# Linear attention with a gated convolution on one core: batch 0's softmax of q by additions in SBUF, batch 1's attention in float32, and a new order of all steps

## The chip, the core and the metric

The kernel runs on one core of one Trainium2 chip. The core has five engines that run side by side, each working through its own instructions strictly in the order in which they were issued: TensorE (PE, matrix products; its weight loads are shown apart as PEld), VectorE (DVE), ScalarE (ACT), GpSimd (POOL) and SyncE (SP), which here only issues DMA transfers. The metric is the device time of one execution in microseconds (us). Three runs of the kernel before gave a median of 322.0 us (321.49 to 322.12).

## What is computed

Eight batches, eight heads, 576 positions (`S`), 64 features per head (`D`), so 512 channels (`C`). All inputs and the output are float32.

```python
q_s = softmax(q, axis=-1)                 # over the 64 features of a head
k_s = softmax(k, axis=2)                  # over the 576 positions
kv  = einsum('bhsd,bhse->bhde', k_s, v)   # 64x64 per head
x   = einsum('bhsd,bhde->bhse', q_s, kv)  # -> (batch, 576, 512)
gate = sigmoid(causal_conv(x, conv_w))    # five taps per channel along the positions
out  = (gate * (x @ w_val)) @ w_out       # two 512x512 products
```

The softmaxes subtract the maximum first and divide by the sum plus 1e-9.

## The kernel before

The two large products are split into three passes each: both operands are cut into a high part (`fp32r`) and the rest, and low x high, high x high and high x low are added up in PSUM (`split_product`, L542). One step `value b m` or `project b m` makes one block of 128 channels of one batch with 24 such matmuls of 288 columns; a batch has four of each.

A batch goes through these stages. Loads of k, q and v. The softmax of k: for batches 0 and 1 from a copy that has channels on the partitions (`load_kc`, `k_top`, `k_raise`, `k_turn`), for the others by maxima of the channels (`load_km`, `k_peak`, L274) that go through memory and come back spread over the partitions (`k_row`, `k_spread`), a subtraction in five parts (`k_sub`, L289) and an exponential (`k_exp`). The softmax of q: maxima (`q_max`, L347), subtraction, exponential, sums (`q_sum`, L362), scaling in four or five parts (`q_mul`, L387 and L389). `kv` (L433) makes the 64x64 blocks, `kv_norm` scales them. `q_turn` transposes q on PE, `q_turned` copies the result to SBUF, and `attend b p` (L498, L499) makes x for 128 channels in PSUM. x is read from PSUM by `x_high` and `x_low` (the two parts for the product), by `first` (the last tap) and four `tap` steps (L524 on DVE; in the other form L527 on ACT and L528 on POOL). After that come `sigmoid`, `value`, `gated` (L563), `g_high` and `g_low` (L571), `project`, and `store`.

PSUM has two buffers of tag `x` and two of tag `mm`. `q_turn` and `attend` take turns in the first pair, so an `attend` can only begin when every reader of an earlier x in its buffer has ended.

The softmax of q in batch 0 is done on PE before the change. `q_peak` transposes the maxima, `q_top` copies them to SBUF, `q_lift` copies q into PSUM by a product with the identity, `q_minus` adds the negative maxima, and `q_raise` takes the exponential out of PSUM. Batch 1 uses `q_neg` and `q_exps` instead: a negated maximum, then either an addition on POOL and one exponential on ACT (letter p), or eight exponentials with a bias on ACT (letter a).

The weights come as pairs of 32-bit words and are put together on the way (`load_words`, `part`, `field`, `scaled`, `signed`, `joined`, then `w_high` and `w_low`): index 0 to 3 are blocks of `w_val`, 4 to 7 of `w_out`, 8 the taps.

In batches listed in `F32_BATCHES` the attention is one float32 product; in the others `kv_high`, `kv_low` and `q_low` cut the operands in two parts and `attend` makes three passes.

What sets the order is a list, `ORDER`, written out by hand: each entry is a step with its batch, its block and, where there is a choice, its engine (a ACT, v DVE, p POOL). The steps are issued in that order, so the place of an entry decides the place of its instructions on their engines, its DMAs in SP's queue among them. `warm n` takes a PSUM buffer and makes n transposes of the identity in it.

## Time and profile before

| what | value |
|---|---|
| median of three runs | 322.0 us |
| the profiled execution, its own time | 320.3 us |
| its span, first to last instruction | 318.5 us |
| mean granted TensorE clock | 0.995 |
| HBM read, written | 41.39 MB, 9.45 MB |
| instructions | 6426 |

The span is what all views of the trace are measured from. The 1.8 us between it and the execution's own time lie around it. A row of a view gives a line of the kernel, an engine, an operation, the tile written and the tiles read; x is a count, the first number the busy time in us, the second the mean in ns of one instruction. A value in square brackets is idle time of the engine ahead of the row with what ended it.

### The profile page before, as it was taken

To read this page: it belongs to the slowest core of one execution; us is meant where nothing else is said; L and a number is where in the kernel's file an instruction comes from. 1 tells how busy PE (TensorE), PEld (TensorE's weight loads), DVE (VectorE), ACT (ScalarE), POOL (GpSimd) and SP (SyncE) were. 2 spreads that over 40 slices of the span, in tenths; PEclk is the share of its full clock that TensorE was granted. 3 is DMA by queue.
4 is the path that set the end of the run, shared out by engine and by line. 5 is a ranking of instruction groups with operands and counts; after the bars stand their busy time and mean duration, and the time that the engine had idled before them with its cause. 6 is when DMAs were issued, how large, how long until landed. Compare 5 with 4: busy or idle time off the path is not lost.

```text
span 318.5 us, 6426 instructions
## 1 busy us (share of the span) xinstructions
PE 297.3 (93%) x2557; PEld 276.4 (87%) x2557; DVE 271.5 (85%) x374; ACT 204.6 (64%) x316; POOL 188.7 (59%) x157
## 2 busy tenths in 40 slices
...
GB/s 250 370 390 174 410 396 199 194 8 175 238 264 264 74 181 139 254 189 112 143 64 313 50 232 283 160 16 355 82 0 37 39 77 2 0 74 76 0 42 108
DMA packets 20525, 51.25 MB, mean 161 GB/s; under 512 B 2832, under 2 KB 7312, under 8 KB 17808
## 3 DMA queue, kind: packets, MB, share of 16 engines
...
q8 instruction: 20, 0.33, 0.4%
q14 instruction: 9, 0.07, 0.1%
HBM read 41.39 MB, written 9.45 MB: 160 GB/s over the span
## 4 chain that ended last, share of the span: by engine, by line
PE 55%; DVE 19%; DMA 16%; issue 4%; ACT 4%; SPq 1%; DVEq 0%; ACTq 0%
PE out L542 22%; PE val L542 20%; DVE gate L524 5%; DMA km<-in_k_strided 5%; PE x L498 4%; PE kv L433 4%; DMA words<-in_w_out 3%; DMA out<-o 2%; DMA q<-in_q 2%; DMA q<-in_q_tail 2%; PE qTps L465 2%; DVE qm L347 2%; DVE g L563 2%; DVE qs L362 2%; DVE kpk L274 2%
## 5 line engine op out<-in xcount | busy, mean ns | idle before, releaser
L524 DVE SCALAR_TENSOR_TENSOR gate<-x,cw,gate 128x575 f32<-128x575 f32 (+3 forms) x99 | 78.0, 807 | 3.3 <-POOL gate L528 1.5
L528 POOL TENSOR_TENSOR gate<-gate,far 128x572 f32<-128x572 f32 (+3 forms) x29 | 39.5, 1363 | 39.2 <-ACT far L527 38.9
L542 PE MATMUL out<-gh,w_out_lo 128*128 128x288 f32 x256 | 57.0, 301 | 0.7 <-ACT gh L160 0.7
L542 PE MATMUL val<-xh,w_val_lo 128*128 128x288 f32 x256 | 56.5, 302 | 0.8 <-DVE o L162 0.7
L542 PE MATMUL out<-gl,w_out_hi 128*128 128x288 f32 x256 | 55.6, 296 | 0.9 <-DVE gl L571 0.9
L542 PE MATMUL val<-xl,w_val_hi 128*128 128x288 f32 x256 | 55.0, 296 | 0.9 <-DVE xl L518 0.9
L542 PE MATMUL out<-gh,w_out_hi 128*128 128x288 f32 x256 | 55.4, 295 | 0.0
L542 PE MATMUL val<-xh,w_val_hi 128*128 128x288 f32 x256 | 54.8, 295 | 0.0
L571 POOL TENSOR_TENSOR gl<-g,gh 128x576 fp32r<-128x576 f32 x25 | 36.8, 1476 | 29.5 <-ACT gh L160 23.1
L542 PEld LDWEIGHTS out<-gl,w_out_hi 128*128 128x128 f32 x256 | 41.4, 188 | 1.4 <-DVE gl L571 1.4
L542 PEld LDWEIGHTS val<-xh,w_val_lo 128*128 128x128 f32 x256 | 40.9, 188 | 1.8 <-DVE o L162 0.9
L542 PEld LDWEIGHTS val<-xl,w_val_hi 128*128 128x128 f32 x256 | 41.2, 188 | 1.2 <-DVE xl L518 1.2
L542 PEld LDWEIGHTS out<-gh,w_out_lo 128*128 128x128 f32 x256 | 41.2, 189 | 1.0 <-ACT gh L160 1.0
L542 PEld LDWEIGHTS out<-gh,w_out_hi 128*128 128x128 f32 x256 | 41.5, 188 | 0.0
L542 PEld LDWEIGHTS val<-xh,w_val_hi 128*128 128x128 f32 x256 | 41.3, 188 | 0.0
L389 POOL TENSOR_TENSOR q<-q,qs 128x512 f32<-128x512 f32 x25 | 26.2, 1070 | 14.7 <-DVE qs L364 14.7
L563 DVE TENSOR_TENSOR g<-val,gate 128x576 f32<-128x576 f32 x32 | 23.9, 749 | 9.9 <-PE val L542 7.3
L527 ACT ACTIVATE far<-x,cw 128x572 f32<-128x572 f32 (+3 forms) x29 | 21.0, 737 | 14.2 <-DVE gate L524 9.3
L160 ACT CAST gh<-g 128x576 fp32r<-128x576 f32 x25 | 16.7, 672 | 17.5 <-DVE g L563 17.4
L160 ACT COPY o<-out 128x576 f32<-128x576 f32 (+1 forms) x22 | 13.5, 618 | 22.1 <-PE out L542 12.1
L531 ACT ACTIVATE gate<-gate 128x576 f32<-128x576 f32 x32 | 21.6, 685 | 6.1 <-DVE gate L524 3.5
L289 POOL TENSOR_TENSOR k<-k,kmax 128x512 f32<-128x512 f32 x18 | 24.9, 1397 | 0.9 <-DMA kmax<-krow 0.9
(103 smaller groups left out, 590.1 us busy)
## 6 DMA issues: line engine op xcount, KB each, us to landing
...
```

Of the source, the lines that this page charges most:

```text
L160: nc.scalar.copy(out=out, in_=in_)
L289: engine(e).tensor_sub(kk[r, cs], kk[r, cs], mx[r, cs])
L389: engine(e).tensor_mul(qq, qq, s.unsqueeze(2).broadcast_to([P, H, D]))
L433: nc.tensor.matmul(acc[h * D:(h + 1) * D, p, :], T["k", b][:, c, cs] if c < 4 else ktz[b % 2][:, cs], T["v", b][:, c, hd] if c < 4 else T[ ...
L498: nc.tensor.matmul(ps[:, :MAIN], a, z, start=(i == 0), stop=(i == len(parts) - 1))
L524: nc.vector.scalar_tensor_tensor(out=a, in0=x, scalar=w, in1=a, op0=ALU.mult, op1=ALU.add)
L527: nc.scalar.activation(part, x, AF.Copy, scale=w)
L528: nc.gpsimd.tensor_add(a, a, part)
L531: nc.scalar.activation(T["gate", b, p], T["gate", b, p], AF.Sigmoid)
L542: nc.tensor.matmul(ps[:, cs], a[:, kb, ms], z[kb][:, cs], start=(kb == 0 and i == 0), stop=(kb == NB - 1 and i == 2),)
L563: nc.vector.tensor_mul(T["g", b, m], T["val", b, m], T["gate", b, m])
L571: engine(e).tensor_sub(T["gl", b, m], T["g", b, m], T["gh", b, m].bitcast(F32))
```

## The change

Four things change. Batch 0's q goes the way that batch 1's goes: the five functions for PE and the tile `minus` are taken out, `q_neg` and `q_exps` are used for batch 0 too. `F32_BATCHES` becomes `(0, 1)`, so batch 1 has no `kv_high`, `kv_low` or `q_low`, and its four `attend` steps are one float32 pass. Steps with one input may name POOL as their engine: `part` 2, 4 and 6, `scaled` 2, `w_high` 0, 1 and 5, `kv_high` three times and `g_high` eleven times do. And `ORDER` is another list throughout: 40 `tap` steps in the ACT and POOL form where there were 29, ten `q_mul` on ACT where there were four, and every engine's instructions in another sequence.

```diff
-F32_BATCHES = (0,)
+F32_BATCHES = (0, 1)
 ORDER = [step.strip() for step in """
-    load_kc 0 1, load_q 0 0 2, load_words 8, k_top 0 1, load_ident, q_lift 0 0, q_max 0 0 2, q_peak 0 0 2,
...
+    load_kc 1 0, load_words 8, field 8, load_kc 0 2, k_top 0 2, scaled 8 a, k_raise 0 2, k_top 1 0, load_words 1,
...
     def load_ident():
         nc.sync.dma_start(out=ident, in_=ident_in)
-        nc.scalar.mul(minus, ident[:H, :H], -1.0)
...
-    def q_peak(b, c0=0, c1=5):
-        c1 = min(c1, q_parts(b))
-        ps = T["qpk", b, c0] = bank(f"qpk_{b}_{c0}", "x")
-        for c in range(c0, c1):
-            nc.tensor.transpose(ps[:H, (c - c0) * P:(c - c0 + 1) * P], T["qm", b][:, c * H:(c + 1) * H], ident)
-
-    def q_top(b, c0=0, c1=5, e="a"):
...
-    def q_lift(b, g):
-        ps = T["qlps", b, g] = bank(f"qlps_{b}_{g}", "x")
-        for i, c in enumerate(q_group(b, g)):
-            nc.tensor.matmul(ps[:, i * C:(i + 1) * C], ident, T["q", b][:, c], start=True, stop=False)
-
-    def q_minus(b, g):
...
-    def q_raise(b, g):
-        c = q_group(b, g)
-        nc.scalar.activation(T["q", b][:, c[0]:c[-1] + 1], T["qlps", b, g][:, :len(c) * C].rearrange("p (c n) -> p c n", n=C), AF.Exp)
...
-    minus = const.tile([H, H], F32, tag="minus", name="minus")
```

Three places of the new order follow, as it was and as it is. First SP's queue up to batch 0's v, the first that `kv 0` needs last. Names carry batch and block: `kc_0_3` is block 3 of batch 0, `words3` the third block of `w_val`, `vt0` the tail of v for batches 0 and 1. Before:

```order
L222 DMA words1_113<-in_w_val 128x4x256
L301 DMA kc_0_3_115<-in_k_channels 128x576
L196 DMA q0_92<-in_q 128x1024
L198 DMA q0_92<-in_q_tail 128x512
L222 DMA words3_125<-in_w_val 128x4x256
L301 DMA kc_0_2_138<-in_k_channels 128x576
L301 DMA kc_1_1_142<-in_k_channels 128x576
L196 DMA q1_147<-in_q 128x2048
L222 DMA words0_152<-in_w_val 128x4x256
L301 DMA kc_1_2_165<-in_k_channels 128x576
L202 DMA v0_170<-in_v 128x2080
L205 DMA vt0_172<-in_v_tail 128x520
```

After:

```order
L196 DMA q0_118<-in_q_tail 128x512
L194 DMA q0_118<-in_q 128x1024
L298 DMA kc_0_1_132<-in_k_channels 128x576
L194 DMA q1_138<-in_q 128x2048
L220 DMA words2_143<-in_w_val 128x4x256
L298 DMA kc_1_2_146<-in_k_channels 128x576
L223 DMA ident_72<-in_ident 128x128
L220 DMA words4_175<-in_w_out 128x4x256
L220 DMA words0_200<-in_w_val 128x4x256
L298 DMA kc_1_3_202<-in_k_channels 128x576
L200 DMA v0_229<-in_v 128x2080
L203 DMA vt0_231<-in_v_tail 128x520
```

Ahead of v0 there now stand two more blocks of weights (five in all with `words1` and `words3`, which come just above these rows) and one more `kc`; `ident` has moved from the fourth place of the queue to the fifteenth.

Second, VectorE from the first tap of batch 0 on (`gate_0_1` is block 1 of batch 0; the widths 575 to 572 tell the taps 3 to 0 apart). Before:

```order
L524 SCALAR_TENSOR_TENSOR gate_0_1_385<-x_0_1_381,cw_74,gate_0_1_385 128x575
L524 SCALAR_TENSOR_TENSOR gate_0_1_385<-x_0_1_381,cw_74,gate_0_1_385 128x574
L524 SCALAR_TENSOR_TENSOR gate_0_1_385<-x_0_1_381,cw_74,gate_0_1_385 128x573
L518 TENSOR_TENSOR xl_0_1_419<-x_0_1_381,xh_0_1_387 128x576
L524 SCALAR_TENSOR_TENSOR gate_0_1_385<-x_0_1_381,cw_74,gate_0_1_385 128x572
L524 SCALAR_TENSOR_TENSOR gate_0_0_417<-x_0_0_399,cw_74,gate_0_0_417 128x575
L518 TENSOR_TENSOR xl_0_0_437<-x_0_0_399,xh_0_0_421 128x576
L524 SCALAR_TENSOR_TENSOR gate_0_0_417<-x_0_0_399,cw_74,gate_0_0_417 128x574
L524 SCALAR_TENSOR_TENSOR gate_0_0_417<-x_0_0_399,cw_74,gate_0_0_417 128x573
L249 TENSOR_SCALAR e4_350<-e4_350 128x512
L250 SCALAR_TENSOR_TENSOR e4_350<-words4_348,e4_350 128x512
L524 SCALAR_TENSOR_TENSOR gate_0_0_417<-x_0_0_399,cw_74,gate_0_0_417 128x572
```

After:

```order
L490 SCALAR_TENSOR_TENSOR gate_0_1_386<-x_0_1_374,cw_73,gate_0_1_386 128x575
L490 SCALAR_TENSOR_TENSOR gate_0_1_386<-x_0_1_374,cw_73,gate_0_1_386 128x574
L484 TENSOR_TENSOR xl_0_1_417<-x_0_1_374,xh_0_1_388 128x576
L490 SCALAR_TENSOR_TENSOR gate_0_0_406<-x_0_0_394,cw_73,gate_0_0_406 128x575
L490 SCALAR_TENSOR_TENSOR gate_0_0_406<-x_0_0_394,cw_73,gate_0_0_406 128x574
L484 TENSOR_TENSOR xl_0_0_429<-x_0_0_394,xh_0_0_414 128x576
L490 SCALAR_TENSOR_TENSOR gate_0_0_406<-x_0_0_394,cw_73,gate_0_0_406 128x573
L271 TENSOR_REDUCE kpk_2_439<-km_2_2_408 128x1
L490 SCALAR_TENSOR_TENSOR gate_0_0_406<-x_0_0_394,cw_73,gate_0_0_406 128x572
L490 SCALAR_TENSOR_TENSOR gate_0_2_489<-x_0_2_484,cw_73,gate_0_2_489 128x575
```

Of block 1 two taps have left VectorE, and one of block 2 (its tap 2); the pair of `signed` that stood inside block 0's taps has moved behind them, and the first maximum of batch 2's k (`kpk_2`) stands there instead.

Third, GpSimd from the subtraction in batch 2's q (`q2`, `qm_2`) to that in batch 2's k (`k2`, `kmax_2`). Before:

```order
L351 TENSOR_TENSOR q2_372<-q2_372,qm_2_689 128x512
L262 TENSOR_TENSOR w_out_lo_78<-f5_518,w_out_hi_77 128x4x128
L571 TENSOR_TENSOR gl_0_1_769<-g_0_1_722,gh_0_1_739 128x576
L254 TENSOR_TENSOR f7_724<-e7_590,f7_724 128x512
L351 TENSOR_TENSOR q2_372<-q2_372,qm_2_689 128x512
L254 TENSOR_TENSOR f6_776<-e6_747,f6_776 128x512
L351 TENSOR_TENSOR q2_372<-q2_372,qm_2_689 128x512
L262 TENSOR_TENSOR w_out_lo_78<-f6_776,w_out_hi_77 128x4x128
L351 TENSOR_TENSOR q2_372<-q2_372,qm_2_689 128x512 x2
L528 TENSOR_TENSOR gate_1_1_773<-gate_1_1_773,far_1_1_0_854 128x572
L262 TENSOR_TENSOR w_out_lo_78<-f7_724,w_out_hi_77 128x4x128
L289 TENSOR_TENSOR k2_693<-k2_693,kmax_2_815 128x512 x2
```

After:

```order
L348 TENSOR_TENSOR q2_554<-q2_554,qm_2_682 128x512 x2
L537 TENSOR_TENSOR gl_0_1_735<-g_0_1_688,gh_0_1_711 128x576
L166 TENSOR_SCALAR f6_738<-words6_384 128x512
L251 TENSOR_TENSOR f6_738<-e6_639,f6_738 128x512
L494 TENSOR_TENSOR gate_1_1_725<-gate_1_1_725,far_1_1_3_769 128x575
L259 TENSOR_TENSOR w_out_lo_77<-f6_738,w_out_hi_76 128x4x128
L348 TENSOR_TENSOR q2_554<-q2_554,qm_2_682 128x512
L251 TENSOR_TENSOR f7_816<-e7_635,f7_816 128x512
L348 TENSOR_TENSOR q2_554<-q2_554,qm_2_682 128x512
L259 TENSOR_TENSOR w_out_lo_77<-f7_816,w_out_hi_76 128x4x128
L286 TENSOR_TENSOR k2_307<-k2_307,kmax_2_855 128x512 x4
L286 TENSOR_TENSOR kt2_372<-kt2_372,kmax_2_855 64x512
```

`TENSOR_SCALAR f6` is a step that ScalarE had. Batch 2's subtraction of q stands between the weights' last steps (`f6`, `f7`, `w_out_lo`) in both; the five instructions of `k_sub` now follow in one run.

More of the change, by code (lines that the diff above doesn't have):

```diff
@@ L68 @@
-    g_high 1 1 a, tap 1 3 0 v, g_low 1 1 v, sigmoid 1 2, value 1 2, gated 1 2, load_km 4 0, warm 0, tail_turn 2,
-    kv_high 2 a, q_turn 2 0, k_sub 3 0 v, k_peak 4 0, tail_turned 2 a, sigmoid 1 3, q_turn 2 1, load_v 3,
-    q_turned 2 0 a, g_low 1 0 p, g_high 1 2 a, q_turned 2 1 a, q_low 2 0, k_sub 3 4 p, load_q 3, kv_low 2 p,
-    g_low 1 2 p, value 1 3, attend 2 1, q_low 2 1, attend 2 0, x_high 2 1 a, gated 1 3, q_max 3, first 2 1 a,
-    g_high 1 3 a, first 2 0 a, k_sub 3 1 p, load_km 4 2, tap 2 0 3 v, x_low 2 1, tap 2 0 2 v, g_low 1 3 p,
@@ L93 @@
-    q_turn 4 0, k_sub 5 3 p, tap 3 3 0 v, q_sub 5 2 p, q_turn 4 1, kv_norm 4 v, kv_high 4 v, value 3 2,
-    q_turned 4 0 a, tail_turned 4 a, kv_low 4 p, value 3 3, q_sub 5 3 p, q_turned 4 1 a, g_low 3 0 p, k_peak 6 1,
-    sigmoid 3 3, q_low 4 0, gated 3 2, q_low 4 1, attend 4 0, gated 3 3, first 4 0 a, attend 4 1, load_km 7 3,
-    g_high 3 2 v, load_q 6, x_high 4 0 a, g_high 3 3 v, g_low 3 2 p, first 4 1 v, q_exp 5, load_k 6, g_low 3 3 p,
-    tap 4 1 3 a, tap 4 0 3 v, x_low 4 0, project 3 2, tap 4 1 2 a, tap 4 0 2 v, x_high 4 1 a, project 3 1,
@@ L133 @@
[L133 to L135 removed]
+    load_kc 1 0, load_words 8, field 8, load_kc 0 2, k_top 0 2, scaled 8 a, k_raise 0 2, k_top 1 0, load_words 1,
+    load_words 3, field 1, signed 8, scaled 1 a, load_kc 0 0, load_kc 0 3, load_q 0 2 5, field 3, part 1 a, signed 1,
```

202 lines of the change are left out of this document (99 added, 103 removed).

## The prediction

> **What bounds the kernel now.** I read the page's busy times first, then the busy time of three stretches.
>
> ```profile
> PE 297.3 (93%) x2557; PEld 276.4 (87%) x2557; DVE 271.5 (85%) x374; ACT 204.6 (64%) x316; POOL 188.7 (59%) x157
> 0.00:45.50 45.50, 33.54 (x277) 20.69 (x277) 37.97 (x66) 35.45 (x65) 22.25 (x26) 0.96 0.90 327
> 45.50:120.60 75.10, 70.22 (x624) 66.79 (x622) 69.06 (x90) 56.10 (x94) 57.70 (x47) 1.00 0.61 188
> 120.60:318.50 197.90, 193.50 (x1660) 188.88 (x1660) 164.50 (x220) 113.00 (x160) 108.72 (x85) 1.00 0.32 112
> ```
>
> The stretches give PE, PEld, DVE, ACT and POOL busy in turn, then clock, DMA share and GB/s. From 120.6 us on PE is busy 193.5 of 197.9 us: little but less matmul work could gain there. Up to 45.5 us DVE is the fullest compute engine (37.97 us), and the DMA engines are 90% busy. Between them PE is the bound, with holes. So the time is the arrival of the first `value`, plus PE's work, plus the holes. The PE timeline shows the arrival and the holes:
>
> ```profile
> 45.55 0.52 PE L542 MATMUL val<-xh,w_val_lo 128*128 128x288 f32 x2
> 65.59 0.53 PE L542 MATMUL out<-gh,w_out_lo 128*128 128x288 f32 x2 [0.65 <-ACT gh L160]
> 67.27 0.54 PE L542 MATMUL out<-gl,w_out_hi 128*128 128x288 f32 x2 [0.90 <-DVE gl L571]
> 82.31 0.54 PE L542 MATMUL val<-xl,w_val_hi 128*128 128x288 f32 x2 [0.93 <-DVE xl L518]
> 84.30 0.53 PE L542 MATMUL val<-xh,w_val_lo 128*128 128x288 f32 x2 [0.66 <-DVE o L162]
> 112.81 0.73 PE L498 MATMUL x<-qT,kvs 128*128 128x512 f32 x2 [1.14 <-ACT far L527]
> ```
>
> The chain that ended last, in order of time, gives what PE's work costs when nothing holds it: 48 matmuls 6.40 us (so a `value` or `project` 3.20), a `kv` 2.48, 16 transposes 1.75, an `attend` 0.70 + 0.17.
>
> ```profile
> 118.10 2.48 PE kv L433 x80
> 120.58 3.41 PE val L542 x24
> 153.50 6.40 PE val L542 x48
> 162.97 1.75 PE qTps L465 x16
> 171.12 0.70 PE x L498 x3
> 171.82 0.17 PE x L499 x2
> ```
>
> From the first `value` (45.55) to batch 2's first (120.58) lie 75.0 us. Both orders have the same steps in it: 16 `value` or `project` (51.2), two `kv` (5.0), four `q_turn` (3.5), a tail (0.4), eight `attend` (7.0), in sum 67.1. So **7.9 us are holes**. The five waits shown are 4.3 of them; the other 3.6 are small waits and restarts. 45.55 and 7.9 are what a new order can change.
>
> **Removed matmuls: 0.** The two large groups of batch 0's q matmuls kept PE busy 6.9 and 5.0 us:
>
> ```profile
> L411 PE MATMUL qlps<-q,ident 128*128 128x512 f32 x10 | 6.9, 825 | 5.7 <-DMA ident<-in_ident 5.7
> L416 PE MATMUL qlps<-minus,qtop 8*128 8x512 f32 x10 | 5.0, 616 | 0.6 <-DVE e L240 0.6
> ```
>
> They lie before 45.5 us, where PE idles 12 us; DVE's work and the loads hide them. Without that cover they would be worth some 12 us.
>
> **Arrival of the first value: -0.7 us.** `value 0 0` follows `attend 0 3`, which waits until block 0's last tap has left its PSUM buffer; so DVE's work up to that tap counts.
>
> ```profile
> 3.62 0.75 DVE L307 TENSOR_REDUCE ktop<-kc 128x1 f32<-128x576 f32 x1 [3.62 <-DMA kc<-in_k_channels]
> 43.59 1.53 DVE L524 SCALAR_TENSOR_TENSOR gate<-x,cw,gate 128x572 f32<-128x572 f32 x2
> 28.46 0.86 DVE L448 TENSOR_TENSOR kvd<-kv,ks 64x256 f32<-64x256 f32 x2
> L249 DVE TENSOR_SCALAR e<-e 128x512 int32<-128x512 int32 x8 | 3.3, 416 | 0.0
> L250 DVE SCALAR_TENSOR_TENSOR e<-words,e 128x512 int32<-128x512 int32 x8 | 5.5, 692 | 0.3
> L162 DVE COPY qtop<-qpk 8x256 f32<-8x256 f32 x1 | 0.4, 412 | 1.0 <-PE qpk L395 1.0
> L274 DVE TENSOR_REDUCE kpk<-km 128x1 f32<-128x576 f32 x24 | 17.7, 742 | 4.1 <-DMA km<-in_k_strided 4.1
> L389 DVE TENSOR_TENSOR q<-q,qs 128x512 f32<-128x512 f32 x7 | 4.8, 684 | 0.0
> L162 DVE CAST qT<-qTps 128x1024 fp32r<-128x1024 f32 x1 | 1.2, 1225 | 0.1
> taps<-in_conv_w SPq DMA_DIRECT2D x1, 20.0 KB, 3.8
> ```
>
> It loses two taps (a pair 1.53), one `signed` (0.42 + 0.69), the scalings of `kv_norm 0` (0.86) and `q_top` (0.41): 3.9. It gains a `k_peak` (0.74), `part` 3 and 8 (0.42 for the large one, by the one-input row of the same shape; the small one I put at 0.15), a `q_mul` (0.68) and a `q_turned` (1.23): 3.2. A small conversion that goes and two negations that come I set equal. Net -0.7. DVE now begins when the taps have landed, about 5.0 us (issued second, 3.8 to land), and not at 3.6; that costs 1.4. The 1.0 us wait for `qpk` goes, and I take 0.4 of the other early waits as swallowed too: together zero.
>
> The loads cost nothing as long as this cover holds:
>
> ```profile
> 12.00:16.00 4.00, 3.77 (x14) 2.48 (x14) 3.93 (x6) 3.42 (x5) 2.53 (x2) 0.57 1.04 419
> 11.84 1.79 PE L319 MATMUL kps<-ident,kc 128*128 128x128 f32 x8
> 21.26 1.04 PE L319 MATMUL kps<-ident,kc 128*128 128x128 f32 x8
> 30.00 1.13 PE L498 MATMUL x<-qT,kvd 128*128 128x512 f32 x2
> 35.75 2.51 DVE L524 SCALAR_TENSOR_TENSOR gate<-x,cw,gate 128x575 f32<-128x575 f32 x3
> 47.20 1.83 ACT L451 ACTIVATE kvd<-kv,ks 64x64 f32<-64x64 f32 x8
> ```
>
> Ahead of `vt0` stand 1312 KB more, at 419 GB/s 3.2 us. `kv 0` followed the transposes of 21.26, at 22.3, with v just landed; now it can begin at 25.5 to 26. With `kv` (2.48), `kv_norm` on ACT (1.83, as batch 1's) and the two ACT steps ahead of that, the first `attend` comes at about 31.9, not 30.0. But DVE reaches its first tap at 35.75 before, and by adding up its new list at 35.8 after. Nearly 6 us of cover shrink to 4, less the 2 or so that `first` and `x_high` need. If it goes, that tap is late next, and with it all of DVE.
>
> **Batch 1 in float32: +1.0 us.**
>
> ```profile
> 39.71 1.12 PE L498 MATMUL x<-qT,kvd 128*128 128x512 f32 x2 [0.70 <-DVE gate L524]
> 40.67 0.33 PE L499 MATMUL x<-qTt,kvd 128*128 128x64 f32 x2
> ```
>
> One float32 pass took 40.67 - 39.71 = 0.96 us on PE, three split passes 0.70. Four times 0.26 is 1.04, all on the bound. In return two `q_low` leave DVE and a `kv_low` leaves POOL; that goes into the holes.
>
> **Holes: 7.9 becomes 5.9, -2.0 us.** I went along PE's new order and asked at each step when its last input is there.
>
> ```profile
> L571 POOL TENSOR_TENSOR gl<-g,gh 128x576 fp32r<-128x576 f32 x25 | 36.8, 1476 | 29.5 <-ACT gh L160 23.1 <-DVE gh L162 6.4
> L389 POOL TENSOR_TENSOR q<-q,qs 128x512 f32<-128x512 f32 x25 | 26.2, 1070 | 14.7 <-DVE qs L364 14.7
> L289 POOL TENSOR_TENSOR k<-k,kmax 128x512 f32<-128x512 f32 x18 | 24.9, 1397 | 0.9 <-DMA kmax<-krow 0.9
> L605 POOL MEMSET kvd<- 128x512 f32 x2 | 1.0, 526 | 0.3 <-POOLq L645 0.3
> ```
>
> `project 0 0` still waits: batch 2's `q_max` stands on DVE ahead of `gated 0 1`, and POOL does two subtractions of q (1.07 each) before `g_low 0 1` (1.48). I make that 2.3 us, against 1.55 in the rows of 65.59 and 67.27. The waits at 82.31 and 84.30 go: the store that held a buffer is on ACT, and DVE has two `q_low` and two taps less. The one at 112.81 goes too: the ACT tap that frees the buffer now has a `project` between it and the `attend`. A new one stands at `kv 3`: from the first `value` to the last `k_sub 3` POOL has 55 us to do (15 sums or products of q 16, six `g_low` 9, ten `k_sub` 13, the weights 12, a tap, `kv_low` and two `g_high` 5), is 4 us behind at the start and waits 4 us for inputs that I can name; `kv 3` is then ready 1.5 us after PE gets there. So 2.3 + 1.5 + 0.2 of small ones, and about half of the unexplained 3.6: 5.9.
>
> One-input work on POOL is in no row. It lies between a fill (0.53) and a two-input pass (1.48), as far from the one as from the other, so I take 1.0. Four such steps on this path make the ends -1.9 and +1.9 us.
>
> [...]
>
> **After 120.6 us: 0.** The work is the same; 4.4 us of idle PE are there to lose or gain. DVE has fewer taps, POOL more in hand: no sign that I can defend.
>
> **Sum:** -0.7 + 1.04 - 2.0 = -1.7. The span of 318.5 becomes 316.8, the profiled execution's 320.3 becomes 318.6; the median of the runs shown is 322.0, so I predict **320.3**.
>
> **Rivals.** (1) *Slower: POOL becomes the bound.* It was busy 57.7 of 75.1 us, and my path leaves it 4 us of waiting. If one input costs 1.48 (+1.9) and it waits 4 more, `kv 3` comes 5.9 later, of which holes elsewhere on PE take up some 1.5: 324.7. Past 1.7 us of such delay the change is slower than before. For it: long waits such as `g_low`'s 29.5. Against: the old order left POOL time to wait; much of that was no need.
>
> (2) *PE's clock is low at the start.* The eight transposes took 1.79 us where the granted clock was 0.57, and 1.04 later. PE now begins with them at about 19 us. At that ratio `kv 0` and q's transposes take 3 us longer, of which 2 are covered, and what follows may lose another: +1 to +2, 321.3 to 322.3. Against: 12 us of idle PE before 45.5 left the clock at 0.96 on average.
>
> [...]
>
> (3) *The holes close*, down to the 2.0 unexplained: -3.9 more, 316.4. (4) *The change doesn't do at the start what it says*: the loads, not DVE, set the first `value`, and the taps that left DVE free nothing; v's 3.2 us less 2 of cover give +1.2 in place of -0.7: 322.2.
>
> **How the numbers follow.** Forecast 0.40, (1) 0.25, (2) 0.10, (3) 0.18, (4) 0.07. A measurement of this kernel tells 0.2%, 0.64 us, from no change. Faster beyond that: three quarters of the forecast, all of (3), some of (2): 0.52. Within: most of (2) and (4), a little of the forecast: 0.18. Slower: (1) and the rest, 0.30. The range leaves out a tenth at each end: 316.0 to 324.5.
>
> **What would show it.** First `value` at 44.9; `kv 0` at 25.5 to 26; batch 2's first `value` at 118.9; batch 1's `attend` at 0.96 + 0.17; no wait before batch 1's second `value`; one-input POOL rows near 1.0 us. Wrong would be: PE idle over 2 us at `kv 2` or `kv 3` behind `k_sub`, a low clock beyond 30 us, or new holes after 120 us, for which I have no term.

## The result and the profile after

The change made the kernel slower. The changed kernel took 323.32 us (median of 16 runs, 322.03 to 325.36), the kernel before 321.56 us beside it (16 runs, 318.31 to 326.47). The ratio is 1.0093, with a 95% interval of 1.0068 to 1.0117. All ratios here leave out executions more than 1.5% above the fastest of their kernel (four of these sixteen of the kernel before, none of the changed one), so they differ from the ratio of the medians, here 1.0055. I had predicted 320.3 us, faster than before. The profiled execution took 322.36 us, its span is 320.4 us; before it was 320.3 and 318.5.

The three stretches again, cut at the first `value` of batch 0 and of batch 2; the columns are PE, PEld, DVE, ACT and POOL busy, then clock, DMA share and GB/s:

```profile
0.00:47.30 47.30, 20.32 (x236) 15.88 (x236) 39.25 (x65) 33.77 (x72) 29.01 (x32) 1.00 0.78 280
47.30:122.00 74.70, 70.05 (x619) 65.95 (x618) 71.31 (x88) 55.94 (x93) 63.99 (x53) 1.00 0.63 216
122.00:320.40 198.40, 193.15 (x1662) 188.75 (x1660) 159.39 (x207) 130.12 (x210) 123.84 (x103) 1.00 0.32 110
```

POOL has 6.8 us more to do than before in the first stretch (29.01 against 22.25) and 6.3 more in the second. DVE has 1.3 us more in the first, where I had forecast less. In the second it is busy 71.31 of 74.70 us: there it is now as full as PE.

PE's timeline, the rows that answer to those of before and the new waits:

```profile
35.61 1.10 PE L464 MATMUL x<-qT,kvd 128*128 128x512 f32 x2 [1.36 <-DVE qT L160]
...
47.34 0.52 PE L508 MATMUL val<-xh,w_val_lo 128*128 128x288 f32 x2
...
63.14 1.09 PE L431 MATMUL qTps<-ident,q 128*128 128x128 f32 x8 [1.16 <-DVE gate L490]
64.95 1.13 PE L464 MATMUL x<-qT,kvd 128*128 128x512 f32 x2 [0.72 <-ACT qT L158]
66.90 1.13 PE L464 MATMUL x<-qT,kvd 128*128 128x512 f32 x2 [0.66 <-ACT qT L158]
72.73 0.54 PE L508 MATMUL out<-gl,w_out_hi 128*128 128x288 f32 x2 [1.49 <-DVE gl L537]
...
122.03 0.42 PE L508 MATMUL val<-xh,w_val_lo 128*128 128x288 f32 x2
```

The first `attend` comes at 35.61 and the first `value` at 47.34, 1.8 us later than before (45.55). Batch 2's first `value` comes at 122.03; in this view it was at 120.51 before. The span's 1.9 us are thus 1.79 up to the first `value`, -0.27 from there to batch 2 (74.69 against 74.96), and 0.38 behind it (198.37 against 197.99).

Why DVE is late shows where its timeline is laid beside POOL's. DVE, from the sum of batch 0's q to its first tap:

```profile
21.71 2.81 DVE L359 TENSOR_REDUCE qs<-q 128x40 f32<-128x2560 f32 x1
...
25.38 0.77 DVE L166 TENSOR_SCALAR f<-words 128x512 int32<-128x512 uint32 x1
26.07 2.44 DVE L237 TENSOR_SCALAR e<-words 128x512 f32<-128x512 f32 x2
28.43 2.54 DVE L386 TENSOR_TENSOR q<-q,qs 128x512 f32<-128x512 f32 x2
...
39.52 1.66 DVE L490 SCALAR_TENSOR_TENSOR gate<-x,cw,gate 128x575 f32<-128x575 f32 x2
```

POOL in the same microseconds:

```profile
24.34 1.52 POOL L166 TENSOR_SCALAR f<-words 128x512 int32<-128x512 uint32 x1
25.95 1.10 POOL L386 TENSOR_TENSOR q<-q,qs 128x512 f32<-128x512 f32 x1
27.00 1.22 POOL L376 TENSOR_TENSOR q<-q,qm 128x512 f32<-128x512 f32 x1
28.19 1.22 POOL L386 TENSOR_TENSOR q<-q,qs 128x512 f32<-128x512 f32 x1
29.38 1.93 POOL L166 TENSOR_SCALAR e<-e 128x512 f32<-128x512 f32 x1
```

Two clamps of the weights (L237) take 2.44 us; before, one took 0.36 to 0.43. Two multiplications of q (L386) take 2.54; before, one took 0.68. No wait stands in front of them: the engine counts as busy, and each of the four, 1.22 or 1.27 us in the mean, lasts about as long as one of POOL's q operations (1.10 to 1.22). That is 2.8 us lost by two rows without any idle time in the profile.

In the kernel before, like operations met POOL's as well, and there it was POOL that lost. DVE's timeline, then POOL's:

```profile
25.07 0.36 DVE L240 TENSOR_SCALAR e<-words 128x512 f32<-128x512 f32 x1
...
26.19 0.69 DVE L389 TENSOR_TENSOR q<-q,qs 128x512 f32<-128x512 f32 x1
...
27.66 0.42 DVE L240 TENSOR_SCALAR e<-words 128x512 f32<-128x512 f32 x1
```

```profile
25.30 3.67 POOL L389 TENSOR_TENSOR q<-q,qs 128x512 f32<-128x512 f32 x3 [1.06 <-DVE qs L364]
```

POOL's three multiplications took 1.04, 1.49 and 1.22 us. The second and the third began at 26.30 and 27.75, some 0.1 us after DVE's operations of 26.19 and 27.66, and those kept their 0.69 and 0.42; between the two DVE had a reduction. In the changed kernel POOL's multiplication began first (25.95), and DVE's four operations follow each other without anything between them. So in these rows the one that begins second waits. e6, below, has one group each way: four clamps took 3.25 us where DVE began first, by 0.7 us, and 4.34 where POOL did.

### The profile page after: what moved, and what is told of

The parts are those of the page before. It is cut to its first block, busy times and chain, and to the rows that moved or that the text cites. A ratio compares the mean times of both kernels' runs of the same rounds, so it can differ in the third digit from the quotient of the medians.

```text
span 320.4 us, 6418 instructions
## 1 busy us (share of the span) xinstructions
PE 283.5 (88%) x2512; PEld 270.6 (84%) x2512; DVE 269.9 (84%) x358; ACT 219.8 (69%) x373; POOL 216.8 (68%) x187
## 4 chain that ended last, share of the span: by engine, by line
PE 61%; DVE 27%; issue 4%; ACT 3%; DMA 2%; SPq 1%; POOL 0%; DVEq 0%; ACTq 0%
PE val L508 25%; PE out L508 22%; PE kv L399 5%; DVE gate L490 5%; PE x L464 4%; DVE qm L344 3%; PE qTps L431 3%; DMA q<-in_q_tail 2%; DVE gl L537 2%; DVE e L237 2%; DVE g L529 2%; DVE qs L359 2%; DVE xl L484 1%; DVE kpk L271 1%; DVE e L246 1%
## 5 line engine op out<-in xcount | busy, mean ns | idle before, releaser
L494 POOL TENSOR_TENSOR gate<-gate,far 128x572 f32<-128x572 f32 (+3 forms) x40 | 53.0, 1326 | 35.4 <-ACT far L493 34.6
L490 DVE SCALAR_TENSOR_TENSOR gate<-x,cw,gate 128x573 f32<-128x573 f32 (+3 forms) x88 | 70.5, 809 | 2.8 <-POOL gate L494 1.7
L493 ACT ACTIVATE far<-x,cw 128x572 f32<-128x572 f32 (+3 forms) x40 | 28.9, 744 | 19.2 <-DVE gate L490 10.3
L537 POOL TENSOR_TENSOR gl<-g,gh 128x576 fp32r<-128x576 f32 x22 | 32.0, 1456 | 8.0 <-ACT gh L158 4.2
L158 ACT COPY o<-out 128x576 f32<-128x576 f32 (+1 forms) x24 | 15.0, 628 | 19.2 <-PE out L508 18.0
L348 POOL TENSOR_TENSOR q<-q,qm 128x512 f32<-128x512 f32 x23 | 25.6, 1127 | 3.3 <-DVE qm L344 2.4
L286 POOL TENSOR_TENSOR k<-k,kmax 128x512 f32<-128x512 f32 x20 | 26.5, 1354 | 1.4 <-DMA kmax<-krow 1.3
L484 DVE TENSOR_TENSOR xl<-x,xh 128x576 fp32r<-128x576 f32 x32 | 23.5, 748 | 0.8 <-ACT xh L158 0.6
```

What stands on the lines that cost most here:

```text
L158: nc.scalar.copy(out=out, in_=in_)
L286: engine(e).tensor_sub(kk[r, cs], kk[r, cs], mx[r, cs])
L348: engine(e).tensor_sub(qq, qq, T["qm", b][:, cs].unsqueeze(2).broadcast_to([P, H, D]))
L484: nc.vector.tensor_sub(xl, T["x", b, p], T["xh", b, p].bitcast(F32))
L490: nc.vector.scalar_tensor_tensor(out=a, in0=x, scalar=w, in1=a, op0=ALU.mult, op1=ALU.add)
L493: nc.scalar.activation(part, x, AF.Copy, scale=w)
```

## Experiments

The theory to test: **an operation of DVE whose operands all lie in SBUF stands still while POOL works**, and the change put more of POOL's work beside such operations. Rivals: the loads set the first `value`; batch 1 in float32 is the loss; TensorE's clock is low. Ratios below are to the kernel before, run beside each, with their 95% intervals.

### e6: operations side by side

Not the kernel: groups of four like operations, first alone, then one group of DVE beside one of POOL.

```python
def together(d, p, first="p"):
    for t in (a, b, a) if first == "p" else (b, a, b):
        nc.scalar.copy(out=t, in_=t)      # both engines wait for this
    for i in range(4):
        if d: d()
        if p: p()
```

> Not the kernel's computation: no attention, convolution or projection is done, only groups of four like operations of VectorE and GpSimd, first each alone, then beside each other, on tiles of 128x512 and 128x576. Theory (a VectorE operation whose operands all lie in SBUF waits for GpSimd's operation at hand): clamp about 0.36 us alone, 0.9 to 1.3 beside GpSimd's multiply; multiply by a broadcast row 0.68 alone, 1.0 to 1.7 beside it; the reduction and the operations that read PSUM (tap 0.8, copy 0.65) change by under 10%. GpSimd's one-input multiply takes 1.5 us or more alone if it is slow by itself, about 0.7 alone if its 1.5 to 1.9 us came from waiting on VectorE. Rival (VectorE was slow for another reason, such as DMA writes into SBUF): every VectorE operation within 10% of its time alone.

DVE's timeline. L53 clamps, L60 multiplies by a broadcast row, L63 reduces, L66 is a tap (one operand in PSUM); the first four rows are alone, the last four beside POOL's multiplication:

```profile
4.93 1.81 DVE L53 TENSOR_SCALAR a<-words 128x512 f32<-128x512 f32 x4 [4.93 <-DMA words<-in_w_val]
...
12.49 2.87 DVE L60 TENSOR_TENSOR a<-a,s 128x512 f32<-128x512 f32 x4 [1.99 <-ACT a L86]
17.29 2.85 DVE L63 TENSOR_REDUCE m<-a 128x1 f32<-128x512 f32 x4 [1.94 <-ACT a L86]
22.14 3.38 DVE L66 SCALAR_TENSOR_TENSOR a<-x,w,a 128x576 f32<-128x576 f32 x4 [2.00 <-ACT a L86]
...
55.08 4.34 DVE L53 TENSOR_SCALAR a<-words 128x512 f32<-128x512 f32 x4 [24.55 <-ACT a L86]
...
67.65 5.41 DVE L60 TENSOR_TENSOR a<-a,s 128x512 f32<-128x512 f32 x4 [1.94 <-ACT a L86]
74.99 2.85 DVE L63 TENSOR_REDUCE m<-a 128x1 f32<-128x512 f32 x4 [1.94 <-ACT a L86]
80.17 3.37 DVE L66 SCALAR_TENSOR_TENSOR a<-x,w,a 128x576 f32<-128x576 f32 x4 [2.34 <-ACT a L86]
```

POOL's timeline, four operations each alone (L72 and L75 multiply by a constant, L79 by a broadcast row, L82 converts), and in the last row L79 beside DVE's L60:

```profile
31.90 6.30 POOL L72 TENSOR_SCALAR b<-words 128x512 int32<-128x512 uint32 x4 [30.02 <-ACT b L86]
38.98 6.20 POOL L75 TENSOR_SCALAR b<-b 128x512 f32<-128x512 f32 x4 [0.79 <-ACT b L86]
45.97 4.40 POOL L79 TENSOR_TENSOR b<-b,s 128x512 f32<-128x512 f32 x4 [0.79 <-ACT b L86]
51.13 2.64 POOL L82 CAST r<-b 128x512 fp32r<-128x512 f32 x4 [0.77 <-ACT b L86]
...
67.12 5.39 POOL L79 TENSOR_TENSOR b<-b,s 128x512 f32<-128x512 f32 x4 [1.69 <-ACT b L86]
```

By fours: the clamp goes from 0.45 to 1.09 us, POOL's own 1.10. The multiplication goes from 0.72 to 1.35, and POOL's from 1.10 to 1.35. The reduction (0.71) and the tap (0.84) don't change. So beside this POOL operation DVE's clamp and multiplication, which go from SBUF to SBUF, are held up; the reduction, though it reads SBUF, and the tap, which reads PSUM, are not. POOL's multiplication by a constant takes 1.55 to 1.58 us by itself, more than its two-input one (1.10).

### e2: two conversions back on ACT

```diff
-    part 2 p, load_k 2,
+    part 2 a, load_k 2,
...
-    scaled 2 p, k_top 1 1,
+    scaled 2 a, k_top 1 1,
```

> The changed kernel with two of its conversions of weight slab 2 (part 2 and scaled 2) on ScalarE instead of GpSimd, which takes 3.45 us of one-input work out of GpSimd's block at 24.3 to 31.3 us. Theory (VectorE stands still while GpSimd works): the clamp pair and the q pair on VectorE together fall from 4.98 us to 3.0 to 4.0, the first value comes 1 to 2 us earlier (45.3 to 46.3), ratio to the kernel before 1.003 to 1.006. Rival (loads): first value within 0.3 us of 47.3, ratio 1.009. Rival (ScalarE's added 1.3 us become the bound): first value later than 47.5.

Ratio 1.003 (0.9995 to 1.0065); median 321.44 us, where the changed kernel had 323.32. DVE's timeline:

```profile
24.50 0.18 DVE L360 TENSOR_SCALAR qs<-qs 128x40 f32<-128x40 f32 x1
...
25.04 0.36 DVE L166 TENSOR_SCALAR f<-words 128x512 int32<-128x512 uint32 x1
25.32 2.44 DVE L237 TENSOR_SCALAR e<-words 128x512 f32<-128x512 f32 x2
27.69 2.13 DVE L386 TENSOR_TENSOR q<-q,qs 128x512 f32<-128x512 f32 x2
...
38.36 1.66 DVE L490 SCALAR_TENSOR_TENSOR gate<-x,cw,gate 128x575 f32<-128x575 f32 x2
```

The first tap comes 1.16 us earlier, and the rows say whence: L166 0.77 to 0.36, the q pair 2.54 to 2.13, and L360 0.47 to 0.18. The clamps stay at 2.44, since POOL's q operations now stand beside them; so the two pairs together came to 4.57 us and not to the 3.0 to 4.0 expected. The first `value` is at 46.18, within what the theory said. `kv 0`'s matmuls ran slow in this execution (1.14 us for 16, against 0.67 in the changed kernel), which didn't undo the gain.

### e14: work that nobody waits for

The kernel **before**, with multiplications of a scratch tile on POOL where it was idle:

```diff
+    def idle(n):
+        for i in range(n):
+            nc.gpsimd.tensor_mul(z, z, z)          # z: 128x256
-    q_mul 0 4 p, joined 0 p, part 2 a,
+    q_mul 0 4 p, idle 4, joined 0 p, idle 4, part 2 a,
```

> The kernel before with eight additional multiplications of a small scratch tile (128x256) on GpSimd, four behind q's last multiplication and four behind joined 0, at 29 to 35 us; nothing reads or waits for that tile, and GpSimd was idle there for 2.4 and 2.9 us. Theory (GpSimd's work holds up VectorE's SBUF operations although neither waits for the other's data): the clamp, signs and copy of VectorE at 29.7 to 35.7 us grow by 1 to 2.5 us together, its first tap comes at 36.7 to 38.3 instead of 35.75, the first value 0.8 to 2.3 us later than 45.55, ratio 1.002 to 1.007. Rival (no such effect in this kernel): first tap within 0.3 us of 35.75, ratio at most 1.001.

Ratio 1.0076 (1.0035 to 1.0117). DVE's timeline:

```profile
31.52 0.48 DVE L240 TENSOR_SCALAR e<-words 128x512 f32<-128x512 f32 x1
31.93 0.83 DVE L249 TENSOR_SCALAR e<-e 128x512 int32<-128x512 int32 x1
32.79 0.98 DVE L250 SCALAR_TENSOR_TENSOR e<-words,e 128x512 int32<-128x512 int32 x1
...
36.49 0.53 DVE L162 CAST w_val_hi<-f 128x512 fp32r<-128x512 f32 x1
36.94 0.83 DVE L249 TENSOR_SCALAR e<-e 128x512 int32<-128x512 int32 x1
37.81 0.98 DVE L250 SCALAR_TENSOR_TENSOR e<-words,e 128x512 int32<-128x512 int32 x1
```

These six took 0.43, 0.42, 0.69, 0.36, 0.41 and 0.69 before, 3.00 together; here 4.63. Neither engine waits for the other's data, so the 1.6 us come from working at the same time. The first tap (39.16) and the first `value` (48.97) came later than either side expected, because the sum of q started at 23.85 in this execution, ahead of all added work: the four matmuls of `q_minus` took 3.74 us here and 1.95 in the first profile of before. Measured from that sum, the first `value` takes 25.12 us, against 23.86 in the first profile of before.

### e3: the loads

```diff
+    load_v 0,
     load_words 4, k_top 0 1, q_exps 0 0 p,
...
     load_words 0, load_kc 1 3,
...
-    load_v 0,
```

> The changed kernel with v of batch 0 (1.3 MB) loaded ahead of weight slabs 4 and 0 instead of behind them. Theory (VectorE, not the loads, sets the first value): kv 0 starts 0.6 to 0.9 us earlier than 25.96, the first value stays within 0.3 us of 47.3, ratio to the kernel before 1.008 to 1.010. Rival (the later load of v sets the first value): first value 0.6 to 0.9 us earlier and ratio about 1.006.

Ratio 1.0106 (1.0054 to 1.0157). `kv 0` starts at 25.46, 0.5 us earlier, and the first `value` at 48.05, 0.7 later and not within the 0.3 of 47.3 that the theory said. The sum of q started later in this execution, at 22.44; from there the first `value` takes 25.61 us, as in the changed kernel (25.63). The loads of v don't set it.

### e4 and e5: one part of the change alone, in the kernel before

e4 has batch 1 in float32, e5 the additions for batch 0's q at the places of the matmuls:

```diff
-F32_BATCHES = (0,)
+F32_BATCHES = (0, 1)
-    kv_high 1 a,
...
-    kv_low 1 p,
...
-    q_low 1 0,
...
-    q_low 1 1,
```

```diff
-    load_ident, q_lift 0 0, q_max 0 0 2, q_peak 0 0 2,
+    load_ident, q_max 0 0 2,
...
-    q_top 0 0 2 v, field 8, load_words 3, q_minus 0 0, scaled 1 a,
+    q_neg 0 0 2, field 8, load_words 3, scaled 1 a,
...
-    q_raise 0 0,
+    q_exps 0 0 p, q_exps 0 1 p,
```

> The kernel before with batch 1's attention in float32 and nothing else: its rounding of kv, its low parts of kv and of q are left out, as in the changed kernel. Rival (float32 is the loss): four attends at 0.97 us instead of 0.70 give 1.04 us, batch 2's first value at 121.6 instead of 120.5, ratio 1.003. Theory (float32 is paid back where VectorE was late): VectorE is rid of two operations of 1.21 us at 58 to 62 us, the holes of 0.8 and 1.0 us in TensorE's work at 65 and 67 us shrink by 1.0 to 1.8 us together, and batch 2's first value comes at 119.7 to 120.7; ratio 0.997 to 1.001.

> The kernel before with batch 0's softmax of q by additions on GpSimd (five of 1.04 us) in place of TensorE's matmuls, at the same places of the order, and nothing else. Theory (the additions cost by standing beside VectorE's SBUF operations and by their own chain): VectorE's clamps, scale and signs at 10 to 22 us grow by 1 to 2 us, first value 46 to 48 instead of 45.55, ratio 1.002 to 1.007. Rival (the additions are free or a gain, and the loss lies in the new order alone): first value at 45.6 or earlier, ratio at most 1.000.

e4: ratio 0.9996 (0.9954 to 1.0038). From the first `value` (45.82) to batch 2's (119.92) it takes 74.10 us where before took 74.96, though PE has 1.04 us more to do. The two waits at 65 and 67 us have become one of 0.53. So in the kernel before float32 is paid back, and it isn't the loss there; no run takes it out of the changed kernel.

e5: ratio 1.0058 (1.0019 to 1.0097), first `value` at 47.18. The loss lies ahead of the sum of q, but less by DVE's clamps than by the chain of additions. DVE's row of that sum, then POOL's of the additions:

```profile
23.73 2.82 DVE L362 TENSOR_REDUCE qs<-q 128x40 f32<-128x2560 f32 x1 [1.88 <-ACT q L380]
```

```profile
19.91 6.05 POOL L379 TENSOR_TENSOR q<-q,qm 128x512 f32<-128x512 f32 x6
```

At the old places the additions come one by one at 1.0 us, and the sum waits 1.88 us for the last exponentials. From the sum to the first `value` it then takes 23.45 us, as in before. The changed kernel's new order loads q earlier and starts that sum at 21.71: it wins this back, and loses its time only behind the sum.

### e1 and e8: another order at 25 to 37 us

DVE's and POOL's steps of the changed kernel from `q_sum 0` on, in another sequence; e8 has e2's move as well:

```diff
 VectorE
-part 3 v, field 0, field 4, q_mul 0 2 v, q_mul 0 3 v, k_top 1 3, scaled 0 v, k_top 1 1, kv_norm 0, signed 0, q_turned 0 0 v, q_sum 1
+q_mul 0 2 v, q_mul 0 3 v, k_top 1 3, kv_norm 0, k_top 1 1, q_turned 0 0 v, q_sum 1, part 3 v, field 0, field 4, scaled 0 v, signed 0
 GpSimd
-q_exps 1 1 p, part 2 p, q_mul 0 4 p, q_exps 1 0 p, q_mul 0 1 p, scaled 2 p, joined 0 p
+q_exps 1 1 p, q_mul 0 4 p, q_mul 0 1 p, q_exps 1 0 p, part 2 p, scaled 2 p, joined 0 p
```

> Same steps on the same engines as the changed kernel; only their order between 25 and 37 us is another: VectorE multiplies q right after the sums and does its reductions while GpSimd is busy, and the clamps, part and scale of the weights come when GpSimd's queue is empty. Theory (VectorE's SBUF operations stand still while GpSimd works): the pair of q multiplications ends by 28.5 us instead of 30.9, the two clamps take under 1.2 us instead of 2.4, the first attend comes at 31.5 to 33 instead of 35.6, the first value at 44.5 to 46.0 instead of 47.3, and the time falls by 1.5 to 2.5 us against the changed kernel (ratio to the kernel before 1.002 to 1.005). Rival (the loads set the first value): first value within 0.3 us of 47.3 and ratio 1.009. Rival (batch 1 in float32 is the loss): ratio 1.009 as well, even if the first value comes earlier.

> Run e1's order together with run e2's move of part 2 and scaled 2 to ScalarE. Theory (VectorE loses time wherever GpSimd works beside its SBUF operations; e1 only moved the meeting to 37 to 39 us and made GpSimd's queue late for the taps at 46 us): with 3.45 us less on GpSimd both go, VectorE's first tap at 36.5 to 38, first value at 44.5 to 45.7, ratio 0.998 to 1.003. Rival (the order makes no difference, only the amount on GpSimd counts): first value as in e2, 46.2, and ratio 1.003.

Both missed: e1 1.0109 (1.0053 to 1.0166), e8 1.0109 (1.0050 to 1.0168). In e1 the first `attend` came at 33.12 and the q pair ended at 27.2 as wanted, the first `value` at 47.02 all the same. DVE's timeline of e1:

```profile
36.90 1.64 DVE L247 SCALAR_TENSOR_TENSOR e<-words,e 128x512 int32<-128x512 int32 x1
38.46 0.83 DVE L237 TENSOR_SCALAR e<-words 128x512 f32<-128x512 f32 x1
```

The meeting only moved: L247 (0.69 unhindered) and L237 now stand beside POOL's `joined 0` and what follows it. And `joined 0` came late. ACT's timeline of e1 has the `first` of block 0 waiting for it, because the weights' tiles `e` and the taps' tiles share the buffers of tag `gate`:

```profile
38.02 0.74 ACT L478 ACTIVATE gate<-x,cw 128x576 f32<-128x576 f32 x1 [0.92 <-POOL f L251]
```

e8 waits for the same, 1.09 us at 39.78. TensorE was slow as well. In e1 the granted clock was 0.63 from 42 to 46 us (1.00 in the changed kernel), 16 matmuls of `kv 1` took 1.09 us in place of 0.64 and the `attend` behind them 1.61 in place of 1.12, and ACT's next `first` waited 1.82 us for it. In e8 the matmuls of `kv 0` (1.14) and of `kv 1` (1.08) both ran slow. So e1's 47.02 and e8's first `value` at 49.03 are made of several things, which these runs don't part.

### e9, e13 and e19: the holes at 61 to 73 us

In e9 block 3's last tap stands ahead of the weights' operations on DVE, with its sigmoid and two products g moved as well. e13 adds e2's move and puts `part 4` and `part 6` on ACT too. e19 is e13 with two low parts of g earlier.

```diff
 e9
-    signed 5, g_high 0 2 a, field 7, load_km 2 0, field 6, q_turn 1 0, g_low 0 2 v, g_low 0 0 p, value 0 3, tap 0 3 0 v,
+    tap 0 3 0 v, signed 5, g_high 0 2 a, sigmoid 0 3, field 7, load_km 2 0, field 6, q_turn 1 0, g_low 0 2 v, g_low 0 0 p, gated 0 1, value 0 3,
 e13, besides
-    part 2 p, scaled 2 p, part 4 p, part 6 p
+    part 2 a, scaled 2 a, part 4 a, part 6 a
 e19, besides
-    g_high 0 3 a, attend 1 0, attend 1 1, first 1 0 a, signed 7, first 1 1 a, x_high 1 0 a, signed 6, q_sub 2 2 p, g_low 0 3 v, q_sub 2 0 p, g_low 0 1 p,
+    g_high 0 3 a, g_low 0 1 p, g_low 0 3 v, attend 1 0, attend 1 1, first 1 0 a, signed 7, first 1 1 a, x_high 1 0 a, signed 6, q_sub 2 2 p, q_sub 2 0 p,
```

> The changed kernel with one place in the middle changed: block 3's last tap of batch 0 (an operation that reads PSUM) stands on VectorE ahead of the signs and clamps of the weights at 56 to 61 us instead of behind them, its sigmoid goes with it, and two products g stand ahead of the maximum of q. The start is as it was: first value 47.3. Theory (operations of VectorE held up by GpSimd delayed that tap, and with it the sigmoid, the copy of batch 1's q and the attends): the holes of TensorE at 61 to 68 us, 1.32 + 0.94 + 0.81 us, shrink to under 1.0 together, the one of 1.65 us at 72 stays or shrinks, batch 2's first value 2 to 3.5 us earlier (118.5 to 120), ratio to the kernel before 0.999 to 1.004. Rival (ScalarE or PSUM set these holes): batch 2's first value at 121.5 to 122.2 and ratio 1.009.

> Runs e2 and e9 together, and two more conversions (part 4 and part 6, 1.5 and 1.6 us on GpSimd) on ScalarE. Theory (GpSimd's work holds up VectorE at 56 to 72 us as it does at the start): first value at 46.2 or earlier, VectorE's signs and clamps at 56 to 72 us lose 1.5 to 2.5 us, the wait of 3.79 us for g's low part at 67 us falls under 2.3, batch 2's first value at 118.5 to 120.5, ratio 0.995 to 1.001. Rival (VectorE's own load, without GpSimd's part, sets that wait): wait of 3 us or more again, ratio 1.002 to 1.006.

> Run e13 with two low parts of g moved: block 1's stands on GpSimd ahead of the first two subtractions of batch 2's q, which wait for VectorE's maximum, and block 3's on VectorE ahead of the signs of the weights. Theory (the hole is made by what stands ahead of g's low part in GpSimd's queue): the wait of 3.02 us at 68.6 us falls under 0.8, batch 2's first value comes 2 to 3.2 us earlier after the first value than e13's 75.7 us, ratio to the kernel before 0.994 to 0.999. Rival (VectorE and GpSimd are full in this stretch, so the hole comes back elsewhere before 122 us): new waits of 1.5 us or more between 66 and 120 us, ratio 1.002 to 1.006.

Ratios: e9 1.0074 (1.0036 to 1.0112), e13 1.0045 (1.0015 to 1.0075), e19 0.9990 (0.9953 to 1.0026). In all three the three waits at 63 to 67 us are gone, so the late tap had made them. But they came back as one, and e9 and e13 missed what the theory expected. PE's timeline of e9, of e13 and of e19:

```profile
70.78 0.85 PE L508 MATMUL out<-gl,w_out_hi 128*128 128x288 f32 x2 [3.64 <-POOL gl L537]
```

```profile
68.59 0.53 PE L508 MATMUL out<-gl,w_out_hi 128*128 128x288 f32 x2 [3.02 <-POOL gl L537]
```

```profile
68.94 0.53 PE L508 MATMUL out<-gl,w_out_hi 128*128 128x288 f32 x2 [0.53 <-DVE gl L537]
74.97 0.67 PE L464 MATMUL x<-qT,kvd 128*128 128x512 f32 x1 [2.30 <-DVE gate L490]
```

In e13 the wait was made by a place in POOL's queue: `g_low 0 1` stood behind two subtractions of q, which wait for DVE's maximum of q. POOL's timeline of e13:

```profile
64.95 2.04 POOL L348 TENSOR_TENSOR q<-q,qm 128x512 f32<-128x512 f32 x2 [2.99 <-DVE qm L344]
66.95 1.58 POOL L537 TENSOR_TENSOR gl<-g,gh 128x576 fp32r<-128x576 f32 x1
```

With that mended in e19, the hole came back 6 us later, now behind a tap of batch 1 on DVE. From the first `value` to batch 2's, e9 took 76.79 us, e13 75.71, e19 75.40, the changed kernel 74.69 to 75.62 in three profiles: no step's place alone shortens the stretch in which DVE is as full as PE. e19 is still the best form of the changed kernel, though against e13 the intervals overlap. Its twelve executions fall into two groups by TensorE's mean clock: seven at 0.989 took 321.45 us in the mean, five at 0.995 to 1.000 took 319.00. Its profile is of the first group, with a granted clock of 0.57 from 76 to 80 us, behind the wait of 2.30; so it doesn't show the faster form, and the clock may be worth 2.4 us there.

### e10, e11 and e15: TensorE's clock

e10 is the changed kernel with 72 unused transposes at places where PE waits, e11 the same in e2. e15 is e4 with the identity loaded first and ten transposes ahead of q's matmuls.

```diff
+EXTRA = {("k_turn", 1, 1): 10, ("k_tail_turn", 1): 12, ("tail_turn", 0): 12, ("attend", 0, 2): 10, ("value", 0, 3): 10, ("attend", 1, 0): 6}
+    def extra(ps, *step):
+        for i in range(EXTRA.get(step, 0)):
+            nc.tensor.transpose(ps, ident, ident)
-    warm 0, q_mul 0 0 a,
+    warm 12, q_mul 0 0 a,
```

```diff
-    load_kc 0 1, load_q 0 0 2, load_words 8, k_top 0 1, load_ident,
+    load_ident, warm 10, load_kc 0 1, load_q 0 0 2, load_words 8, k_top 0 1,
```

> The changed kernel with 62 transposes of the identity added on TensorE, their results unused, at seven places where TensorE waits in the changed kernel's trace (ahead of kv 0, q's and k's transposes, kv 1, the fourth attend, and twice at 61 to 66 us). Theory (besides the stalls of VectorE, most executions of the changed kernel lose 1 to 2 us because TensorE is so idle before 75 us that its clock falls to half for some microseconds; runs e1, e2, e3, e8 and e9 show such stretches, the changed kernel's own profile by chance none): granted clock at 1.00 from 24 to 88 us, ratio to the kernel before 1.003 to 1.007. Rival (the clock costs nothing that counts, since TensorE waits anyway): ratio 1.009 or, with the transposes in the way, up to 1.013.

> Run e2 (two conversions of weight slab 2 on ScalarE) with the same 62 transposes as run e10. Theory (two causes that add up: GpSimd's work beside VectorE, and the clock): clock 1.00 from 24 to 88 us, first value at 46.2 or earlier, ratio 0.997 to 1.002. Rival (the clock costs nothing that counts): ratio as in e2, 1.003, or more.

> Run e4 (the kernel before with batch 1's attention in float32) with the identity loaded first and ten transposes of it put on TensorE ahead of q's first matmuls, their results unused. Theory (in many executions of the kernel before, TensorE's matmuls for the softmax of q run at half clock up to 10 to 14 us and hold up the sums of q): the four matmuls of q_minus at 10 us take 1.95 us or less, VectorE's sum of q starts at 21.7 or earlier and without a wait over 0.5 us, ratio to the kernel before 0.992 to 0.998. Rival (the loads and VectorE set the start, whatever TensorE's clock): sum of q at 21.7 to 22.5, ratio 0.999 to 1.002.

The clock did stay up (mean 0.999 in e10, 1.000 in e11), and the time got worse: e10 1.0162 (1.0124 to 1.0199), e11 1.0104 (1.0063 to 1.0145). That alone doesn't clear the clock, since the transposes can cost time themselves: from the first `value` (46.62) to batch 2's e10 takes 77.6 us, the changed kernel 74.7. But from the sum of q (20.99) to the first `value` e10 takes 25.63 us, the same as the changed kernel. And of the changed kernel's sixteen executions the seven with a mean clock of 1.000 took 323.6 us in the mean, the nine others 323.2. So the clock isn't the changed kernel's loss. The pair repeats e2: with the two conversions on ACT, 0.6% less, in another setting. (The expectations count 62 transposes; with the table's 60 and `warm 12` they are 72.) e15 came to 1.0021 (0.9986 to 1.0056) and settles nothing: the identity ahead made q land later, its first maximum starting at 6.47 us and not at 5.27, and the four matmuls of `q_minus` at 11.36 us still took 3.75; the sum of q came at 24.80, later than either side expected.

### e12, e16, e17 and e18: how typical the profiles are

> The changed kernel itself once more, for a second profile. Theory (its first profile fell on an execution without a fall of the clock, which is the exception): granted clock under 1.00 in at least one stretch of 4 us between 24 and 80 us, mean under 0.992, profiled time 323 us or more, ratio 1.007 to 1.012. Rival (its clock does not fall): mean clock 1.00, as in the first profile, 322.4 us.

> The kernel before once more, for its profile. Theory (its start hangs on when TensorE's clock rises, and its first profile was a fortunate one): the four matmuls of q_minus take 3.7 us, the sum of q starts at 22.3 to 24, the first value comes at 46.2 to 48, span 319 to 321. Rival (first profile is typical, and the whole 1.8 us at the first value is the change's): sum of q at 21.7, first value at 45.3 to 45.8, span 318.2 to 318.8.

> The kernel before a third time, for its profile; expectations as for e16: q_minus 3.7 us, sum of q at 22.3 to 24, first value at 46.2 to 48 by the theory; 1.95 us, 21.7 and 45.3 to 45.8 by the rival.

> The changed kernel a third time, for its profile. Its start holds no matmuls for q: both theories expect the sum of q at 21.2 to 21.8, q's pair of multiplications and the two clamps on VectorE at 4.5 to 5.1 us together, the first value at 46.7 to 47.5, span 320.4 to 321.8.

e12, which was also timed, gave 323.47 us and 1.0102 (1.0066 to 1.0138). Moments in us, from the timelines:

| profile | sum of q | first tap | first `value` | batch 2's first `value` | span | sum to first `value` |
|---|---|---|---|---|---|---|
| before | 21.69 | 35.75 | 45.55 | 120.51 | 318.5 | 23.86 |
| before, e16 | 22.92 | 36.59 | 46.39 | 120.87 | 319.0 | 23.47 |
| before, e17 | 21.93 | 35.84 | 45.65 | 122.65 | 321.4 | 23.72 |
| after | 21.71 | 39.52 | 47.34 | 122.03 | 320.4 | 25.63 |
| after, e12 | 21.21 | 39.01 | 46.83 | 122.45 | 321.5 | 25.62 |
| after, e18 | 21.16 | 38.98 | 46.80 | 121.82 | 320.4 | 25.64 |

The last column is the steadiest: the changed kernel takes 1.8 to 2.2 us longer from the sum of q to the first `value`, every time. Its sum starts 0.8 us earlier in the mean (21.36 against 22.18). In e16 DVE waited 1.48 us ahead of the sum for the exponentials that come behind PE's matmuls, in e17 0.81, in the first profile not at all: that one was fortunate. The cause that I expected for this wasn't seen: `q_minus` took 1.95 us in e16 and e17 too, and not 3.7; and the fall of the clock expected in e12 didn't come (mean 1.000). In the mean of three the first `value` is 1.1 us later, the stretch to batch 2 0.4 shorter, the rest 0.4 longer: 1.1 us in all, against 1.8 and 2.4 between the medians. The remaining microsecond isn't located by these profiles.

No kernel here beats both: e19 (0.999), e4 (0.9996) and e2 (1.003) are level with the kernel before. What the best experiments on the changed kernel win back is about what it had lost.

## Why the prediction was wrong

**The step that failed: "Arrival of the first value: -0.7 us".** It came out at +1.8. It added up DVE's new list at the durations of before's rows, in which DVE hadn't been held up though POOL was at work beside some of them, and got a first tap at 35.8; it came at 39.52. The list was right and the durations weren't. Between the sum of q and the first tap lie 17.81 us, where before has 14.06. Of the 3.75, 1.7 are the two clamps, 1.2 the two multiplications, 0.4 L166 and 0.3 L360, in sum 3.6; what else differs in the two lists nearly cancels. e6 and e14 show that POOL holds up operations of these kinds, and e2 releases a part of them. The first `value` moved less than the tap because fewer taps of DVE stand ahead of it. I had priced POOL's work by how long it keeps POOL, and left out what it does to DVE.

The measured 323.32 lies within the 316.0 to 324.5 that I gave, but by luck: the upper end came from rival (1), whose mechanism didn't occur.

**Holes: -2.0, measured -1.3.** From the 74.69 us I take 67.1 of work and 1.04 for float32: 6.5 us of holes, from 7.9. The waits at 82, 84 and 112 us went, as written. The wait at `project 0 0` was 1.49, not 2.3. The 1.5 at `kv 3` didn't come. In their place stand three that I hadn't seen (1.16, 0.72 and 0.66 at 63 to 67 us), behind a tap that stood on DVE after the weights' operations; e9 shows that.

**One input on POOL at 1.0 us** was between two prices: conversions take 0.61 to 0.79 us in the changed kernel (two of them 1.06 and 1.13), multiplications by a constant 1.5 to 1.9.

**Batch 1 in float32: +1.04** held to the row (0.97 + 0.17 for an `attend`), and e4 shows that the freed operations pay it back. **Removed matmuls: 0** was read from a fortunate profile; in the mean the sum of q starts 0.8 us earlier without them, though the new order of the loads may have its part in that, and no run separates the two. **After 120.6: 0** came out at +0.4, within what profiles of one kernel differ by (198.0 to 198.8 in before).

**The loads.** `kv 0` began at 25.96, as written, and the cover held, as e3 shows; the first `attend` was 3.7 us later than the 31.9 worked out, for the q pair that ended at 31.0 on DVE.

**Rivals.** (1) put the right engine in the wrong place: POOL's own queue never made `kv 3` late, it slowed DVE. (2) was right that TensorE starts slow: the changed kernel's first sixteen transposes took 3.64 us at 20.03, where eight took 1.04 at 38.18. But `kv 0` then waited another 1.43 us for v, so that was covered; and e10 kept the clock up without gain. (4) fell by e3, and (3) by e9, e13 and e19, which show the holes moving, not closing. So the chance that I gave to slower (0.30) stood, in the main, on a mechanism that didn't occur.
